# Counting the SBUF port that VectorE and GpSimd share in a kernel's own scheduler

## The chip, the cores and the metric

The kernel runs on one core of a Trainium2 chip. The metric is the device time of one execution in microseconds. A core has TensorE (matrix products), VectorE, ScalarE and GpSimd (elementwise work) and SyncE, which here issues the DMAs. GpSimd reads and writes SBUF only; the results of matmuls lie in PSUM and are read by VectorE and ScalarE.

## The reference

Causal attention with a bias from running sums, then two feed-forward layers, all in 32-bit floats, for 4 sequences of 576 tokens, 8 heads of 64:

```python
scores = (q @ k^T) / sqrt(64)
cum    = cumsum(max(s, 0))
scores = where(causal, -1e9, scores + min(-(cum[:, None] - cum[None, :]), 0))
attn   = exp(scores - rowmax); attn = attn / (rowsum + 1e-9)
x      = attn @ v                              # 2304 tokens x 512
x      = ((x @ w_a) * (x @ w_b)) @ w_out       # 512 -> 1536 -> 512
h      = x @ w_in                              # 512 -> 2048
out    = (max(h, 0) + alpha * min(h, 0)) @ w_out2
```

## The kernel before

**Tiles and stages.** The 2304 tokens are cut into four blocks of 512 and a last one of 256. For each block, `ffn(blk)` (L901) runs both feed-forward layers; between its matmuls the steps of the attention of the next block are interleaved (`attention(blk)`, L738). The attention of the first sequence runs alone at the start (`first_attention`, L693). TensorE's work is in its own order in the program text.

**Exact products.** A 32-bit product is made of three products of split operands (`mm3`, L893): each operand is split into a high part and a low part by `split` (L266): a copy into the type fp32r, mostly on ScalarE (L239), and a subtraction `lo = src - hi` (L252, `sub`). For weights these are the tiles wh and wl, for gated activations gh and gl, for the layer's input xh and xl. wl and gl are computed from SBUF, so VectorE or GpSimd can do them; xl is computed from PSUM, so VectorE does it.

**Weights.** There are 68 weight tiles of 128x512. They arrive as 64-bit floats. While block 0 is computed, `decode` (L802) turns each into 32-bit: one scaling on ScalarE (L810) or GpSimd (L812), then on VectorE one shift (a TENSOR_SCALAR w<-w) and two combines (SCALAR_TENSOR_TENSOR w<-raw,w), all three issued through `dve` (L245). The result sits in one of four w32 buffers until it is split and stored to the DRAM tensor w_d; blocks 1 to 4 read it back from there (raw<-w_d). The buffers of wh and wl are six each.

**Softmax.** Per head and row block: VectorE reduces scores out of PSUM (L245, z<-bank), ScalarE takes the exponential (L232), VectorE makes the reciprocal of the sums (sm), and `scale` (L257) multiplies the rows by it, on GpSimd or VectorE. `scale` also multiplies by alpha in the second layer (m). GpSimd masks the diagonal (L490). In later blocks VectorE or ScalarE adds the bias (L480, L484).

**The order of the work.** Everything that is not TensorE's is a chain of steps (Python generators). A step yields a dictionary of engines with a planned duration in ns, and the class `Order` simulates them while the program is being built: `_first` (L121) takes the step that can start earliest, ties going to the earlier due time, and `_run` (L136) emits it on an engine. So the scheduler fixes each engine's instruction order and, where a dictionary names two engines, which of them gets the instruction. The first engine of a dictionary is kept unless another one would end the step sooner by more than `late`: 1000 ns (LATE), 1300 ns in block 0 (LATE_0). Each engine is a resource of its own: `free[e]` is when it is next free. On the chip the engines run these orders and wait for each other by semaphores.

Of the kernel before, what the change touches and what calls it, by code (L numbers as in the profile page):

```python
# [13 lines left out]
ALU = mybir.AluOpType  # L14
# [10 lines left out]
SIGN = -(1 << 31)  # L25
# [47 lines left out]
        self.free, self.waiting = n, []  # L73


class Order:


# [42 lines left out]
    def _first(self):  # L121

        best = None
        for link in self.open:
            due, n, c, (engines, _) = link
            end, late = None, 0.0
            for e, t in engines.items():
                at = max(c.time, self.free.get(e, 0.0)) + t
                if end is None or at + late < end:
                    end, eng, start = at, e, at - t  # L130
                late = self.late
            if best is None or (start, due, n) < best[:3]:
                best = start, due, n, link, eng, end
        return best

    def _run(self, first):  # L136
        _, _, _, link, eng, end = first
        self.open.remove(link)
        c, (_, wait) = link[2:]
        self.free[eng] = end  # L140
        c.time = end + wait
        self._next(c, eng)

# [29 lines left out]
def attention_two_moe_kernel(  # L173
# [10 lines left out]
    nc = tc.nc  # L184
# [7 lines left out]
    WN = 512  # L192
# [25 lines left out]
            engines={ENGINES.PE, ENGINES.Activation, ENGINES.DVE, ENGINES.Pool, ENGINES.SP}  # L218
# [6 lines left out]
    SEEN = 100  # L225

    def size(ap):
        return prod(ap.shape[1:])

    def act(o, i, func=AF.Copy, **k):  # L230
        yield {"act": 90 + 0.833 * size(o) + 93 * len(set(k) - {"scale"})}, SEEN
        nc.scalar.activation(o, i, func, **k)  # L232

    def copy(o, i, rate):

        n = size(o)
        eng = yield {"act": 90 + 0.833 * n, "dve": 70 + rate * n}, SEEN
        if eng == "act":
            nc.scalar.activation(o, i, AF.Copy)  # L239
        else:  # L240
            nc.vector.tensor_copy(o, i)

    def dve(n, rate, f, *args, **k):
        yield {"dve": 70 + rate * n}, SEEN
        f(*args, **k)  # L245

    def sub(o, i0, i1, sbuf=True):
        n = size(o)
        engines = {"pool": 115 + 2.17 * n} if sbuf else {}
        engines["dve"] = 70 + 1.04 * n  # L250
        eng = yield engines, SEEN
        (nc.vector if eng == "dve" else nc.gpsimd).tensor_tensor(o, i0, i1, op=ALU.subtract)  # L252

    def scale(o, i, s0, s1):
        n = size(o)
        eng = yield {"pool": 115 + 1.09 * n, "dve": 70 + 0.52 * n}, SEEN
        (nc.vector if eng == "dve" else nc.gpsimd).tensor_scalar(  # L257
            o, i, s0, s1, op0=ALU.mult, op1=ALU.mult
        )

# [186 lines left out]
    def z_space(r, b, h):  # L447

        if b == 0 and r < 4 and h // 2 % 3 == 2:
            return {0: (gp, "gh", 3), 2: (gp, "gl", 3), 3: (ft, "t", 4)}[r] + (of_early[r],)  # L450
        return work, f"z{r}", 1 if r == 4 else 4, of_z[r]

    def biases(b, h, rs):

        r = rs[-1]
        got = []
        first = b < SUMS_PE and r < 4
        cb, ready = (None, None) if first else cb_t[b, h, r // 4]  # L460
        col = b * H // 2 + h if r == 4 else b * H + h
        pool, tag, bufs, slots = z_space(rs[0], b, h)

        def chain():
            if not first:
                yield ready
            yield slots
            z = pool.tile([P, sum(min(S, P * (i + 1)) for i in rs)], F32, name="z", tag=tag,
                          bufs=bufs)
            got.append(z)  # L470
            c = 0
            if first:
                return
            for i in rs:
                n = min(S, P * (i + 1))
                o, q = z[:, c:c + n], cumq[:, i, col:col + 1]
                both = {"act": 180 + 0.833 * n, "dve": 70 + 0.52 * n}
                eng = yield dict(sorted(both.items(), reverse=not scarce)), SEEN
                if eng == "dve":
                    nc.vector.tensor_scalar(  # L480
                        o, cb[0][:, 0:n], q, 0.0, op0=ALU.add, op1=ALU.min
                    )
                else:
                    nc.scalar.activation(o, cb[0][:, 0:n], AF.Identity, bias=q)  # L484
                c += n
            if r >= 3:
                run.give(of_c1 if r == 4 else of_c0, run.t)

            def keep(d, pattern):
                nc.gpsimd.affine_select(  # L490
                    d, d, pattern=pattern, base=0, channel_multiplier=1, compare_op=ALU.is_ge,
                    fill=MASKED,
                )

            if r == 4:
                for j in range(2):
                    yield {"pool": 120 + 1.09 * QB}, SEEN
                    keep(z[j * QB:(j + 1) * QB, QA:S], [[-1, QB]])
            else:
                k = len(rs)  # L500
                yield {"pool": 120 + 1.09 * P * k}, SEEN
                d = z.rearrange("p (c n) -> p c n", n=P)
                keep(d[:, 0:3:2, :] if k == 2 else d[:, r:r + 1, :], [[0, k], [-1, P]])

        z_t[b, h, rs[0]] = got, run.spawn(chain(), slack=SL_BIAS)

    def both(b, hp, rs):
# [3 lines left out]
    def soften(b, h, rs, srcs, *banks_read):  # L511

        got, masked = z_t[b, h, rs[0]]
        run.need(masked)
        z = got[0]
        k = len(rs)
        mn = small.tile([P, 2], F32, name="mn", tag="mn")
        sm = small.tile([P, 2], F32, name="sm", tag="sm")
        parts = []
        c = 0  # L520
        for i in rs:
            n = min(S, P * (i + 1))
            parts.append(z[:, c:c + n])
            c += n

        def rest():
            for i, p in enumerate(parts):
                yield from act(
                    p, p, AF.Exp, bias=mn[:, i:i + 1], scale=-1.0, accum_out=sm[:, i:i + 1]
                )  # L530
            for i in range(k):
                yield from dve(
                    1, 1, nc.vector.tensor_scalar, sm[:, i:i + 1], sm[:, i:i + 1], 1e-9, None,
                    op0=ALU.add,
                )
            yield from dve(1, 1, nc.vector.reciprocal, sm[:, 0:k], sm[:, 0:k])
            for i, p in enumerate(parts):
                yield from scale(p, p, sm[:, i:i + 1], 1.0)

        def first():  # L540
            c = 0
            for i, src in enumerate(srcs):
                n = src.shape[-1]
                p = z[:, c:c + n]
                yield from dve(
                    n, 1.04, nc.vector.tensor_tensor_reduce, p, src,
                    mask[:, QA - n:] if b < SUMS_PE and rs[0] < 4 else p, -0.125, BIG, ALU.add,
                    ALU.min, mn[:, i:i + 1],
                )
                c += n  # L550
            if len(parts) < len(srcs):
                yield from dve(
                    1, 1, nc.vector.tensor_tensor, mn[:, 0:1], mn[:, 0:1], mn[:, 1:2],
                    op=ALU.min,
                )
            z_t[b, h, rs[0]] = z, run.spawn(rest(), run.t)

        got = run.spawn(first())
        z_t[b, h, rs[0]] = z, got
        for i in banks_read:  # L560
            reader[i] = got
# [240 lines left out]
    def decode(r, w):  # L802

        r2 = r.rearrange("p (n t) -> p n t", t=2)
        low, high = r2[:, :, 0], r2[:, :, 1]
        wf = f32(w)
        ts, stt = nc.vector.tensor_scalar, nc.vector.scalar_tensor_tensor
        eng = yield {"act": 517, "pool": 590}, SEEN
        if eng == "act":
            nc.scalar.activation(wf, high.bitcast(F32), AF.Copy, scale=REBIAS)  # L810
        else:
            nc.gpsimd.tensor_scalar(  # L812
                wf, high.bitcast(F32), REBIAS, 1.0, op0=ALU.mult, op1=ALU.mult
            )
        yield from dve(WN, 0.52, ts, w, w, 3, None, op0=ALU.logical_shift_left)
        yield from dve(WN, 1.04, stt, w, high, SIGN, w, op0=ALU.bitwise_and, op1=ALU.bitwise_or)
        yield from dve(
            WN, 1.04, stt, w, low, 29, w, op0=ALU.logical_shift_right, op1=ALU.bitwise_or
        )

    def load_pair(i):
# [199 lines left out]
    for blk in range(NB):  # L1021
# [8 lines left out]
        if 1 <= blk < NB - 1:  # L1030
            n = max(0, blk * S + QA - blocks[blk + 1][0])
# [4 lines left out]
        for i, _ in enumerate(ffn(blk)):  # L1036
            want = min(len(steps), (i + 1) * len(steps) * FASTER / total)
            while done < want:
                f, args = steps[done]
# [64 lines left out]
```

## Time and profile before

| | |
|---|---|
| time, median of 3 runs | 1090.11 us (1083.55 to 1091.57) |
| the profiled execution: its time / its span | 1084.09 / 1082.3 us |
| TensorE busy | 1040.2 us, 96% of the span |
| VectorE busy | 564.4 us, 52% |
| ScalarE busy | 568.0 us, 52% |
| GpSimd busy | 661.2 us, 61% |
| subtractions (L252) on GpSimd: wl from w / wl from raw / gl | 56 / 215 / 90 |

The span runs from the first to the last instruction. PE is TensorE, DVE VectorE, ACT ScalarE, POOL GpSimd, SP SyncE, L252 a line of the program. An instruction's busy time runs from its start to its end, and time in which it is held up after its start counts as busy. Busy spans of neighbours on one engine can overlap a little, since the end of one and the start of the next do.

### The profile page before, as it was taken

Reading aid. Unit: us, or ns where it says so; the run is one execution under the profiler, and the core shown is the slowest. Engines: PE = TensorE matmul, PEld = TensorE weight load, DVE = VectorE, ACT = ScalarE, POOL = GpSimd, SP = SyncE. Lnnn points to the kernel's source line nnn. Section 1 sums busy time; section 2 is a strip of 40 time slices with the busy share of each in tenths; the row PEclk is TensorE's granted clock in tenths of the full one; section 3 lists DMA queues with packets and bytes.
Section 4 is the critical chain, followed back from the end, with each engine's and each line's share of the span. In section 5 each row is a group of like instructions: output and inputs, shape, how many; then the busy total and the mean of one; then the engine's idle time right before and its main releaser. Section 6 shows DMA issues by size and latency. Waiting matters only on the chain.

```text
span 1082.3 us, 15995 instructions
## 1 busy us (share of the span) xinstructions
PE 1040.2 (96%) x5413; PEld 817.5 (76%) x5413; DVE 564.4 (52%) x1233; ACT 568.0 (52%) x1187; POOL 661.2 (61%) x664
## 2 busy tenths in 40 slices
PE   6889899888999999999999999999999999999998
PEld 5467677666777777777777777777788888889987
DVE  6989889889835333543445343543222233433443
ACT  6755555655555545554455445455443444446564
POOL 3666536566767545666566655655544456667997
PEclk9989999989999999999999999999999999999999
DMA  7675856745667243435256343423163243216551
GB/s 221 203 238 180 279 210 220 259 167 200 220 187 224 82 136 103 134 105 161 59 147 181 74 145 96 137 81 111 49 202 126 88 129 98 79 58 234 182 169 40
DMA packets 87394, 162.68 MB, mean 150 GB/s; under 512 B 7120, under 2 KB 24528, under 8 KB 87312
## 3 DMA queue, kind: packets, MB, share of 16 engines
q1 hardware_dynamic: 87312, 161.66, 47.0%
q8 instruction: 42, 0.69, 0.3%
q14 instruction: 40, 0.33, 0.1%
HBM read 139.02 MB, written 22.62 MB: 149 GB/s over the span
## 4 chain that ended last, share of the span: by engine, by line
PE 74%; DVE 11%; issue 6%; POOL 5%; ACT 2%; DMA 1%; SPq 0%; POOLq 0%; DVEq 0%; ACTq 0%
PE bank L894 17%; PE bank L895 16%; PE bank L896 16%; DVE w L245 7%; PE bank L1003 5%; PE bank L1005 5%; PE bank L1004 5%; PE bank L439 3%; PE bank L633 3%; POOL wl L252 3%; PE bank L613 2%; DVE z L245 1%; PE bank L586 1%; PE bank L682 1%; POOL m L257 1%
## 5 line engine op out<-in xcount | busy, mean ns | idle before, releaser
L252 POOL TENSOR_TENSOR wl<-raw,wh 128x512 fp32r<-128x512 f32 x215 | 280.2, 1309 | 164.8 <-ACT wh L239 144.5
L894 PE MATMUL bank<-xh,wh 128*128 128x512 f32 (+1 forms) x800 | 306.8, 384 | 0.4 <-DVE g L245 0.4
L896 PE MATMUL bank<-xh,wl 128*128 128x512 f32 (+1 forms) x800 | 296.3, 370 | 0.0
L895 PE MATMUL bank<-xl,wh 128*128 128x512 f32 (+1 forms) x800 | 295.8, 370 | 0.0
L239 ACT ACTIVATE wh<-raw 128x512 fp32r<-128x512 f32 x266 | 166.8, 627 | 107.9 <-PE bank L895 50.7
L894 PEld LDWEIGHTS bank<-xh,wh 128*128 128x128 f32 x800 | 151.3, 189 | 40.3 <-issue 13.9
L896 PEld LDWEIGHTS bank<-xh,wl 128*128 128x128 f32 x800 | 151.3, 189 | 26.6
L895 PEld LDWEIGHTS bank<-xl,wh 128*128 128x128 f32 x800 | 151.5, 189 | 23.1
L252 POOL TENSOR_TENSOR gl<-g,gh 128x512 fp32r<-128x512 f32 (+1 forms) x90 | 118.3, 1314 | 46.4 <-ACT gh L239 46.3
L257 POOL TENSOR_SCALAR z<-z,sm 128x128 f32<-128x128 f32 (+4 forms) x133 | 90.4, 689 | 85.8 <-DVE sm L245 58.4
L239 ACT ACTIVATE gh<-g 128x512 fp32r<-128x512 f32 (+1 forms) x140 | 82.2, 587 | 91.4 <-DVE g L245 90.8
L245 DVE SCALAR_TENSOR_TENSOR w<-raw,w 128x512 int32<-128x512 int32 x136 | 128.4, 951 | 2.6
L245 DVE SCALAR_TENSOR_TENSOR g<-bank,m 128x512 f32<-128x512 f32 (+1 forms) x80 | 50.9, 636 | 131.9 <-POOL m L257 131.8
L1003 PE MATMUL bank<-wh,gh 128*128 128x512 f32 x288 | 117.6, 408 | 0.2 <-ACT gh L239 0.2
L1005 PE MATMUL bank<-wh,gl 128*128 128x512 f32 x288 | 113.7, 395 | 0.4 <-POOL gl L252 0.2
L1004 PE MATMUL bank<-wl,gh 128*128 128x512 f32 x288 | 113.3, 393 | 0.0
L252 POOL TENSOR_TENSOR wl<-w,wh 128x512 fp32r<-128x512 f32 x56 | 84.5, 1511 | 44.3 <-ACT wh L239 38.8
L245 DVE TENSOR_TENSOR g<-bank,a_sb 128x512 f32<-128x512 f32 (+1 forms) x60 | 38.1, 635 | 140.7 <-PE bank L896 131.3
L232 ACT ACTIVATE z<-z,mn 128x128 f32<-128x128 f32 (+4 forms) x144 | 82.9, 578 | 52.6 <-DVE mn L245 52.5
L257 POOL TENSOR_SCALAR m<-m,alpha_sb 128x512 f32<-128x512 f32 (+1 forms) x78 | 59.9, 768 | 60.9 <-ACT m L232 60.3
L894 PE MATMUL bank<-gh,wh 128*128 128x512 f32 (+1 forms) x240 | 93.5, 390 | 2.9 <-ACT gh L239 2.9
L895 PE MATMUL bank<-gl,wh 128*128 128x512 f32 (+1 forms) x240 | 89.3, 372 | 2.5 <-POOL gl L252 1.5
(77 smaller groups left out, 1469.3 us busy)
## 6 DMA issues: line engine op xcount, KB each, us to landing
raw<-w_d SPq DMA_DIRECT2D x136, 512.0 KB, 3.9
raw<-in_w_dram SPq DMA_DIRECT2D x68, 512.0 KB, 4.4
w_d<-w SPq DMA_DIRECT2D x68, 256.0 KB, 2.3
kq<-in_kq_a_dram SPq DMA_DIRECT2D x32, 256.0 KB, 5.3
vb<-in_v_dram SPq DMA_DIRECT2D x32, 256.0 KB, 5.2
kq<-in_kq_b_dram SPq DMA_DIRECT2D x16, 352.0 KB, 4.3
cb<-cum_d SPq DMA_DIRECT2D x32, 144.0 KB, 5.8
out_dram<-o SPq DMA_DIRECT2D x18, 256.0 KB, 2.6
```

The costliest lines, as they stand in the source:

```text
L232: nc.scalar.activation(o, i, func, **k)
L239: nc.scalar.activation(o, i, AF.Copy)
L245: f(*args, **k)
L252: (nc.vector if eng == "dve" else nc.gpsimd).tensor_tensor(o, i0, i1, op=ALU.subtract)
L257: (nc.vector if eng == "dve" else nc.gpsimd).tensor_scalar(o, i, s0, s1, op0=ALU.mult, op1=ALU.mult)
L439: nc.tensor.matmul(dst[j], got[0][o, QA + r * P:QA + n], got[0][o, 0:n], start=b >= SUMS_PE, stop=True)
L894: nc.tensor.matmul(o, wh, ih, start=first, stop=False)
L895: nc.tensor.matmul(o, wh, il, start=False, stop=False)
L896: nc.tensor.matmul(o, wl, ih, start=False, stop=last)
L1003: nc.tensor.matmul(acc[t], gh[:, c], wh, start=first, stop=False)
L1004: nc.tensor.matmul(acc[t], gh[:, c], wl, start=False, stop=False)
L1005: nc.tensor.matmul(acc[t], gl[:, c], wh, start=False, stop=last)
```

## The change

A second resource, "port", is held in the plan together with the engine: every GpSimd step holds ("pool", "port"), and a new name for VectorE, "dve2", holds ("dve", "port"). Steps of VectorE that read SBUF on both sides, or copy or scale within SBUF, are now called "dve2": the decode's shift and combines, subtractions and scalings from SBUF, the bias of L480, the copy within SBUF and the minimum of two columns. Those that read PSUM stay "dve". For subtractions and scalings the fixed `late` is replaced by 0.95 of the difference between the two planned durations.

```diff
+HOLDS = {"pool": ("pool", "port"), "dve2": ("dve", "port")}
+class Either(dict):
+    @property
+    def late(self):
+        return 0.95 * (self["pool"] - self["dve2"])
+def holds(e):
+    return HOLDS.get(e, (e,))
@@ Order._first
             for e, t in engines.items():
-                at = max(c.time, self.free.get(e, 0.0)) + t
+                at = max(c.time, *(self.free.get(x, 0.0) for x in holds(e))) + t
                 if end is None or at + late < end:
                     end, eng, start = at, e, at - t
-                late = self.late
+                late = getattr(engines, "late", self.late)
@@ Order._run
-        self.free[eng] = end
+        for x in holds(eng):
+            self.free[x] = end
@@ helpers
     def copy(o, i, rate):
...
-        eng = yield {"act": 90 + 0.833 * n, "dve": 70 + rate * n}, SEEN
+        vector = "dve" if rate > 1 else "dve2"
+        eng = yield {"act": 90 + 0.833 * n, vector: 70 + rate * n}, SEEN
...
-    def dve(n, rate, f, *args, **k):
-        yield {"dve": 70 + rate * n}, SEEN
+    def dve(n, rate, f, *args, port=False, **k):
+        yield {"dve2" if port else "dve": 70 + rate * n}, SEEN
...
     def sub(o, i0, i1, sbuf=True):
         n = size(o)
-        engines = {"pool": 115 + 2.17 * n} if sbuf else {}
-        engines["dve"] = 70 + 1.04 * n
-        eng = yield engines, SEEN
-        (nc.vector if eng == "dve" else nc.gpsimd).tensor_tensor(o, i0, i1, op=ALU.subtract)
+        t = 70 + 1.04 * n
+        eng = yield Either(pool=115 + 2.17 * n, dve2=t) if sbuf else {"dve": t}, SEEN
+        (nc.gpsimd if eng == "pool" else nc.vector).tensor_tensor(o, i0, i1, op=ALU.subtract)
     def scale(o, i, s0, s1):
...
-        eng = yield {"pool": 115 + 1.09 * n, "dve": 70 + 0.52 * n}, SEEN
+        eng = yield Either(pool=115 + 1.09 * n, dve2=70 + 0.52 * n), SEEN
@@ biases (L477)
-                both = {"act": 180 + 0.833 * n, "dve": 70 + 0.52 * n}
+                both = {"act": 180 + 0.833 * n, "dve2": 70 + 0.52 * n}
@@ soften: minimum of two columns
-                    op=ALU.min,
+                    op=ALU.min, port=True,
@@ decode: the shift and both combines
-        yield from dve(WN, 0.52, ts, w, w, 3, None, op0=ALU.logical_shift_left)
+        yield from dve(WN, 0.52, ts, w, w, 3, None, op0=ALU.logical_shift_left,
+                       port=True)
...
```

## Rows read from the trace of the kernel before

**Rows 1.** Windows: stretch, its length; each engine's busy us (instructions); clock; DMA.
```profile
core 0: us, PE busy (x) PEld busy (x) DVE busy (x) ACT busy (x) POOL busy (x), PEclk, DMA share, GB/s
60.00:320.50 260.50, 238.68 (x1167) 182.17 (x1167) 222.79 (x382) 147.79 (x302) 160.38 (x135) 0.97 0.64 216
30.00:307.00 277.00, 250.50 (x1267) 186.09 (x1267) 244.12 (x455) 163.53 (x349) 170.91 (x149) 0.96 0.66 221
320.50:976.60 656.10, 655.62 (x3214) 511.93 (x3213) 251.02 (x611) 317.02 (x643) 380.29 (x402) 1.00 0.39 117
976.60:1082.30 105.70, 99.96 (x727) 93.40 (x725) 43.93 (x58) 61.94 (x129) 91.39 (x82) 0.99 0.47 160
```

**Rows 2.** First feed-forward matmul (L895); output stores of blocks 0 and 1 (start, us).
```profile
L895 PE MATMUL bank<-xl,wh x800: 280/389/628, 60.1 to 1072.8; 128*128 128x512 f32 x128, 128*128 128x256 f32 x32
...
320.54 1.75 SPq L263 DMA_DIRECT2D out_dram<-o  x3
...
550.23 1.99 SPq L263 DMA_DIRECT2D out_dram<-o  x3
```

**Rows 3.** Groups by shape, VectorE, 30 to 307 us: count | busy us, mean ns | idle before.
```profile
L245 DVE SCALAR_TENSOR_TENSOR w<-raw,w 128x512 int32<-128x512 int32 x136 | 128.4, 951 | 2.6
L245 DVE TENSOR_SCALAR w<-w 128x512 int32<-128x512 int32 x68 | 44.4, 655 | 12.3 <-ACT w L810 12.0 <-POOL w L812 0.4
L252 DVE TENSOR_TENSOR wl<-w,wh 128x512 fp32r<-128x512 f32 x12 | 17.8, 1498 | 5.2 <-ACT wh L239 5.1
...
L252 DVE TENSOR_TENSOR gl<-g,gh 128x512 fp32r<-128x512 f32 x4 | 4.6, 1148 | 0.4 <-ACT gh L239 0.4
```

**Rows 4.** Instructions of tiles w and g, whole span: ns min/median/max, first and last start.
```profile
L245 DVE SCALAR_TENSOR_TENSOR w<-raw,w x136: 666/693/1783, 34.4 to 306.6; 128x512 int32<-128x512 int32 x136
L245 DVE TENSOR_SCALAR w<-w x68: 402/421/1520, 34.0 to 305.4; 128x512 int32<-128x512 int32 x68
...
L252 DVE TENSOR_TENSOR wl<-w,wh x12: 716/1366/3110, 47.9 to 300.7; 128x512 fp32r<-128x512 f32 x12
...
L245 DVE SCALAR_TENSOR_TENSOR g<-bank,m x80: 423/691/695, 209.6 to 1075.6; 128x512 f32<-128x512 f32 x64, 128x256 f32<-128x256 f32 x16
```

**Rows 5.** Timeline: start us, us, engine, line, operation (VectorE, then GpSimd).
```profile
182.84 3.11 DVE L252 TENSOR_TENSOR wl<-w,wh 128x512 fp32r<-128x512 f32 x1 [0.54 <-ACT wh L239]
...
182.85 1.29 POOL L252 TENSOR_TENSOR wl<-w,wh 128x512 fp32r<-128x512 f32 x1
184.10 1.29 POOL L252 TENSOR_TENSOR gl<-g,gh 128x512 fp32r<-128x512 f32 x1
```

**Rows 6.** Windows of L252 on GpSimd alone: stretch, length, busy us (instructions).
```profile
30.00:307.00 277.00, 115.69 (x77) 0.96 0.66 221
...
307.00:976.60 669.60, 282.32 (x219) 1.00 0.38 117
```

**Rows 7.** Windows of L257 on GpSimd alone.
```profile
30.00:307.00 277.00, 48.07 (x58) 0.96 0.66 221
```

**Rows 8.** Timeline of VectorE: a combine and the instruction behind it.
```profile
146.06 0.69 DVE L245 SCALAR_TENSOR_TENSOR w<-raw,w 128x512 int32<-128x512 int32 x1
146.67 0.15 DVE L245 TENSOR_SCALAR sm<-sm 128x1 f32<-128x1 f32 x1
```

**Rows 9.** Waits (60 to 320.5 us; last row VectorE's, 30 to 307): us, times, longest.
```profile
ACT w L810 <- POOL wl L252: 43.9, 33, 2.6
...
DVE w L245 <- ACT w L810: 12.0, 11, 2.3
...
DVE wl L252 <- ACT wh L239: 5.1, 6, 1.2
```

**Rows 10.** Waits of TensorE and its weight loads for GpSimd, 0 to 60 us.
```profile
PEld bank L613 <- POOL z L257: 7.2, 6, 2.8
...
PE bank L613 <- POOL z L257: 4.2, 2, 2.6
```

**Rows 11.** Timeline of TensorE: the last matmul.
```profile
1078.11 0.39 PE L1005 MATMUL bank<-wh,gl 128*128 128x512 f32 x1
```

More of the change, by code (lines that the diff above doesn't have):

```diff
@@ L248, in sub @@
         n = size(o)
-        engines = {"pool": 115 + 2.17 * n} if sbuf else {}
-        engines["dve"] = 70 + 1.04 * n
-        eng = yield engines, SEEN
-        (nc.vector if eng == "dve" else nc.gpsimd).tensor_tensor(o, i0, i1, op=ALU.subtract)
+        t = 70 + 1.04 * n
+        eng = yield Either(pool=115 + 2.17 * n, dve2=t) if sbuf else {"dve": t}, SEEN
+        (nc.gpsimd if eng == "pool" else nc.vector).tensor_tensor(o, i0, i1, op=ALU.subtract)
     def scale(o, i, s0, s1):
         n = size(o)
-        eng = yield {"pool": 115 + 1.09 * n, "dve": 70 + 0.52 * n}, SEEN
-        (nc.vector if eng == "dve" else nc.gpsimd).tensor_scalar(
+        eng = yield Either(pool=115 + 1.09 * n, dve2=70 + 0.52 * n), SEEN
+        (nc.gpsimd if eng == "pool" else nc.vector).tensor_scalar(
             o, i, s0, s1, op0=ALU.mult, op1=ALU.mult
@@ L476, in chain @@
                 o, q = z[:, c:c + n], cumq[:, i, col:col + 1]
-                both = {"act": 180 + 0.833 * n, "dve": 70 + 0.52 * n}
+                both = {"act": 180 + 0.833 * n, "dve2": 70 + 0.52 * n}
                 eng = yield dict(sorted(both.items(), reverse=not scarce)), SEEN
-                if eng == "dve":
+                if eng == "dve2":
                     nc.vector.tensor_scalar(
@@ L814, in decode @@
             )
-        yield from dve(WN, 0.52, ts, w, w, 3, None, op0=ALU.logical_shift_left)
-        yield from dve(WN, 1.04, stt, w, high, SIGN, w, op0=ALU.bitwise_and, op1=ALU.bitwise_or)
+        yield from dve(WN, 0.52, ts, w, w, 3, None, op0=ALU.logical_shift_left,
+                       port=True)
+        yield from dve(WN, 1.04, stt, w, high, SIGN, w, op0=ALU.bitwise_and, op1=ALU.bitwise_or,
+                       port=True)
         yield from dve(
-            WN, 1.04, stt, w, low, 29, w, op0=ALU.logical_shift_right, op1=ALU.bitwise_or
+            WN, 1.04, stt, w, low, 29, w, op0=ALU.logical_shift_right, op1=ALU.bitwise_or,
+            port=True
         )
```

## The prediction

> **What bounds the kernel now.** I read the views in this order: busy time by stretch, the groups of instructions by shape, the spread of single instructions, the waits, and last the end of the chain. By stretch [rows 1], TensorE is busy 655.62 of the 656.10 us between 320.5 and 976.6, and 99.96 of the 105.70 us after that. So only the first 320 us have room. Token block 0 runs from 60.1 to 320.5, which is 260.4 us; block 1 takes 229.7 us [rows 2] for the same matrix work without the short matmuls of L429 and L433, for which I allow some 4 us by estimate. About 26 us is therefore all that block 0 can give. TensorE is idle 260.50 - 238.68 = 21.8 us of it, and its granted clock is 0.97 there and 1.00 later. In block 0 each of the 68 weight tiles is also decoded on VectorE: one shift and two combines. From 30 to 307 us VectorE is busy 244.12 of 277 us, and GpSimd 170.91.
>
> VectorE's busy time there is not all work. A combine (SCALAR_TENSOR_TENSOR w<-raw,w) lasts 951 ns in the mean [rows 3], but half of all 136 last 693 ns or less, and the longest 1783 [rows 4]. The gate's product, of the same 128x512 size with one operand in PSUM, never passes 695 ns [rows 4]. So what stretches is the instruction with its operands in SBUF. [rows 5] show one case: a subtraction on VectorE begins at 182.84, two GpSimd subtractions run from 182.85 to 185.39, and VectorE's ends at 185.95, after 3.11 us instead of 0.72.
>
> **The change, part by part.** It adds no instruction and drops none; it reorders them and moves subtractions (L252) and scalings (L257) from GpSimd to VectorE. Before, GpSimd kept one unless VectorE would end it 1000 ns sooner (1300 in block 0). Now VectorE takes it if it ends sooner by more than 0.95 of the planned difference: 592 ns for 128x512, where the difference is 623. Both wait for the same port in the plan, so VectorE takes all that become ready unless it is itself in an instruction that needs no port (reductions from PSUM, gates, small columns). Of VectorE's 244.12 us in the stretch the groups of [rows 3], which use the port, are 195; the other 49 are under a fifth of 277. So I let GpSimd keep a fifth. The other marks (decode, the minimum of two columns, the bias of L480) tell the plan of the port and move nothing by themselves. SyncE issues the same transfers; a subtraction that ends sooner frees its raw or w32 buffer sooner, and the DMA engines, at 0.64 of their time in block 0 [rows 1], have room for a load that starts earlier.
>
> *Block 0, stall that goes.* Against the uncontended durations: combines 136 x (951 - 693) = 35.1 us; shifts 68 x (655 - 421) = 15.9; weight subtractions 12 x (1498 - 716) = 9.4; gl 4 x (1148 - 716) = 1.7 [rows 3, 4]. Together 62 us of VectorE time.
>
> *Block 0, work that comes.* GpSimd has 77 subtractions and 58 scalings there, 115.69 and 48.07 us [rows 6, 7]. Four fifths are 62 and 46. A full-size two-operand instruction on VectorE steps by 146.67 - 146.06 = 0.61 us when it meets nobody [rows 8]; the busy 0.69 overlaps the next. 62 x 0.61 = 38 us. A full-size scaling is like the shift, 0.42 us; the softmax ones are a quarter to four quarters of that width, so 0.35 in the mean by estimate, 46 x 0.35 = 16. Together 54 us.
>
> *Block 0, stall that stays.* Lower bound 0: the chip keeps to the planned order. Upper bound: the two engines meet by chance as now. GpSimd's time falls to a fifth, and VectorE's instructions on the port rise from 220 to 328, so 62 x 0.2 x 1.49 = 18 us. I take 6, nearer to 0: the plan's prices (602 and 1226 ns) are close to the steps measured (0.61 us here, 184.10 - 182.85 = 1.25 on GpSimd [rows 5, 8]), so the planned order should mostly hold. VectorE's sum is -62 + 54 + 6 = -2 us, between -8 and +10.
>
> Here a rule can be weighed. The row shows that VectorE's subtraction lost 3.11 - 0.72 = 2.39 us behind two GpSimd instructions in a row [rows 5]. The Trainium skill (SBUF — State Buffer, Who interferes with whom) calls the shared pair an exclusive lock: the one that starts first has it for its whole instruction and the other blocks, so a wait would end with the instruction in its way. By the rule this wait would have been at most 1.25 us, half of it; the stall that stays would halve with it, to 3 us, and the whole sum would be 1069 in place of 1072 us. The row decides.
>
> *Block 0, waits.* ScalarE's first decode step waits 43.9 us for GpSimd's weight subtraction, which frees one of four w32 buffers, and VectorE's shift waits 12.0 us for that step [rows 9]. The subtraction shrinks from 1.5 to about 0.7 us, and the 12.0 us come as 11 waits of 1.1 us: I take 9 of the 12 off (bounds 0 and 12). Against it, a subtraction on VectorE waits there for ScalarE's wh, with reductions, gates and decodes queued behind it, and TensorE's PSUM banks behind those. The 12 now on VectorE waited 5.1 us, 0.43 each [rows 9]. For 50 more weight subtractions that is 21 us at most, and 0 where VectorE is late anyway. VectorE is busy 88% of the stretch, so I take 3. Block 0 comes to -2 - 9 + 3 = -8 us.
>
> *First attention (0 to 60).* TensorE's transposes and their loads wait 7.2 + 4.2 = 11.4 us for scalings on GpSimd [rows 10]. On VectorE one takes about half as long, but from 30 us on it also decodes there. I take -3 (bounds -6 and 0).
>
> *Blocks 1 to 3: nothing.* 0.8 of 219 subtractions [rows 6] at 0.61 us put 107 us more on VectorE, which is then busy some 360 of 656 us. TensorE covers it; without that cover each wait at the head of VectorE's queue would cost its 0.43 us.
>
> *Last block.* It has half as many tokens per weight, and GpSimd is busy 91.39 of 105.70 us [rows 1] beside a nearly full TensorE. The last matmul ends at 1078.5 of 1082.3 [rows 11], and that tail of 3.8 us stays. Of the 5.74 us idle, about 2 are left: I take -1 (0 to -2).
>
> **Sum.** -8 - 3 + 0 - 1 = -12 us on the profiled execution's own 1084.09 us: 1072 us. That execution is 6 us below the median of the three runs (1090.11), so a median may stand a few us above the sum.
>
> **Rivals.** *The order holds fully.* No stall stays, waits in front of VectorE vanish, and block 0 comes down to TensorE's own pace: -26 - 3 - 1 = -30, 1054 us. For it: the port's load in the plan falls by more than half of GpSimd's 164 us. Against: VectorE still has 244 - 62 + 54 = 236 us of work in 277.
>
> *VectorE is as full as before: no change.* Stall is only exchanged for work (-62 + 54 + 8), the shorter decode loop is eaten by the waits for ScalarE: 1084 us, with 1080 to 1090 around it. For it: the first three terms nearly cancel. Against: the buffer waits of [rows 9] and the first attention. The Trainium skill speaks for this one (Perfetto Trace Analysis, Optimizing Scalar/DVE Operations): the two engines share a port, so "offloading operations between those two might not help". The trace agrees that they block each other; it does not show yet what moving work the other way gives.
>
> *Slower: VectorE queues behind ScalarE.* If each moved weight subtraction holds VectorE for its full 0.43 us (+21) and the stall stays at the chance level (+18 in place of 6), block 0 comes to -62 + 54 + 18 - 9 + 21 = +22 us, less 4 elsewhere: 1102 us. It decides from the point where those waits pass 11 us with the rest of my sum. For it: VectorE is the fuller of the two engines and now gets more. Against: planned times agree with measured ones, and a late VectorE does not wait.
>
> **How the numbers follow.** Forecast 0.46, order holds fully 0.16, no change 0.22, slower 0.16. About 1% (11 us) is what a measurement of this kernel can tell from no change. My forecast lies just past that line; two thirds of its chance is beyond it (0.31) and a third within (0.15). Faster by over 1%: 0.31 + 0.16 = 0.47. Slower by over 1%: 0.15. Within: 0.38. The forecast's own range, by its bounds, is 1060 to 1080. The range for 8 in 10 reaches to the full-order case, 1054, and into the slower one, to 1094.
>
> **What would show it.** In the new profile: combines at 0.69 to 0.75 us in the mean rather than 0.95; GpSimd under 250 us busy in all, VectorE near 700; 50 or more weight subtractions on VectorE before 307 us; block 0's first output before 312 us; blocks 1 to 3 unchanged at 656 us within 2. I would be wrong if combines stayed above 0.85 us (order not kept), if VectorE's waits for ScalarE's wh passed 11 us in block 0, or if TensorE lost its full load after 320 us.

## The result, and the profile after

The changed kernel takes 1053.76 us (median of four runs, 1050.13 to 1055.80) beside 1089.57 for the kernel before. The ratio is 0.9677, with a 95% interval from 0.9627 to 0.9726: 35 us faster. The forecast was 12 us, 1072; the time lies a quarter of a microsecond below 1054, the lower end of the range for 8 in 10. The profiled execution has a span of 1048.4 us.

The same windows as in [rows 1], cut at the new block ends (stretch, length; busy us and count of each engine; clock; DMA):

```profile
core 0: us, PE busy (x) PEld busy (x) DVE busy (x) ACT busy (x) POOL busy (x), PEclk, DMA share, GB/s
0.00:60.00 60.00, 49.22 (x326) 34.29 (x327) 48.88 (x210) 45.25 (x125) 13.28 (x30) 0.97 0.74 210
30.00:280.00 250.00, 245.50 (x1302) 185.10 (x1299) 226.40 (x557) 167.38 (x356) 44.16 (x47) 1.00 0.76 242
56.50:290.30 233.80, 230.64 (x1167) 177.57 (x1167) 210.53 (x479) 149.68 (x304) 43.02 (x46) 1.00 0.76 245
...
290.00:943.00 653.00, 653.00 (x3203) 510.02 (x3202) 362.11 (x866) 317.80 (x643) 110.42 (x146) 1.00 0.39 118
943.00:1048.40 105.40, 101.38 (x738) 95.97 (x737) 67.24 (x128) 63.44 (x130) 15.65 (x13) 1.00 0.50 160
```

The first feed-forward matmul (an answer by tile: ns min/median/max, first and last start in us), then SyncE's timeline with the first stores of blocks 0, 1 and 3, against [rows 2]:

```profile
L916 PE MATMUL bank<-xl,wh x800: 278/389/398, 56.5 to 1040.0; 128*128 128x512 f32 x128, 128*128 128x256 f32 x32
```

```profile
290.32 1.93 SPq L281 DMA_DIRECT2D out_dram<-o  x3
...
520.01 2.62 SPq L281 DMA_DIRECT2D out_dram<-o  x3
...
945.70 1.69 SPq L281 DMA_DIRECT2D out_dram<-o  x3
```

The reader sees where the time went. The stage ahead of block 0 ends at 56.5 us in place of 60.1 (-3.6). Block 0 takes 290.3 - 56.5 = 233.8 us in place of 260.4 (-26.6). Blocks 1 to 3 take 655.4 us, as before (656.1), with TensorE busy 653.00 of 653.00. From the store of block 3 to the end there are 102.7 us in place of 105.7 (-3.0). In block 0 TensorE is now nearly full and its granted clock is 1.00. Of the 26.6 us, 18.6 are idle time of TensorE that is gone (21.8 us before [rows 1], 3.2 now); the other 8.0 are its own busy time, 238.68 us before and 230.64 now for the same 1167 matmuls, with the granted clock at 0.97 before.

VectorE's groups by shape, 30 to 280 us, against 30 to 307 before ([rows 3]; the window ends one decode short: 67 of 68 shifts, 134 of 136 combines); then GpSimd's:

```profile
L264 DVE SCALAR_TENSOR_TENSOR w<-raw,w 128x512 int32<-128x512 int32 x134 | 91.6, 705 | 0.1
L270 DVE TENSOR_TENSOR wl<-w,wh 128x512 fp32r<-128x512 f32 x43 | 30.4, 716 | 3.5 <-ACT wh L258 3.4
L264 DVE TENSOR_SCALAR w<-w 128x512 int32<-128x512 int32 x67 | 27.5, 420 | 5.9 <-ACT w L828 5.8
L270 DVE TENSOR_TENSOR gl<-g,gh 128x512 fp32r<-128x512 f32 x24 | 18.2, 760 | 1.1 <-ACT gh L258 0.9
...
L270 POOL TENSOR_TENSOR wl<-w,wh 128x512 fp32r<-128x512 f32 x23 | 31.3, 1363 | 164.1 <-ACT wh L258 149.5 <-PE bank L604 10.5 <-DMA w_d<-w 3.9
L270 POOL TENSOR_TENSOR gl<-g,gh 128x512 fp32r<-128x512 f32 x2 | 2.6, 1322 | 5.1 <-ACT gh L258 5.1
```

A combine takes 705 ns (before 951), a shift 420 (655), a weight subtraction on VectorE 716 (1498). GpSimd has 25 of the subtractions left there and is busy 44.16 us; before it was 170.91 in the longer stretch.

### The profile page after: what moved, and what is told of

It is laid out like the page before. It is cut to its first block, busy times and chain, and to the rows that moved or that the text cites. A ratio compares the mean times of both kernels' runs of the same rounds, so it can differ in the third digit from the quotient of the medians.

```text
span 1048.4 us, 15810 instructions
## 1 busy us (share of the span) xinstructions
PE 1030.4 (98%) x5413; PEld 814.8 (78%) x5413; DVE 685.0 (65%) x1664; ACT 572.4 (55%) x1192; POOL 180.1 (17%) x228
## 4 chain that ended last, share of the span: by engine, by line
PE 85%; DVE 8%; DMA 4%; ACT 1%; issue 1%; SPq 0%; POOL 0%; ACTq 0%; DVEq 0%; POOLq 0%
PE bank L915 19%; PE bank L917 18%; PE bank L916 18%; PE bank L1024 6%; PE bank L1026 6%; PE bank L1025 5%; PE bank L457 3%; DVE w L264 3%; PE bank L631 3%; DMA w_d<-w 3%; PE bank L651 2%; PE bank L604 1%; DVE z L264 1%; PE bank L700 1%; DVE wl L270 1%
## 5 line engine op out<-in xcount | busy, mean ns | idle before, releaser
L270 DVE TENSOR_TENSOR wl<-raw,wh 128x512 fp32r<-128x512 f32 x209 | 145.0, 695 | 153.6 <-ACT wh L258 150.3
L270 POOL TENSOR_TENSOR wl<-raw,wh 128x512 fp32r<-128x512 f32 x63 | 82.0, 1302 | 333.4 <-ACT wh L258 317.2
L270 DVE TENSOR_TENSOR gl<-g,gh 128x512 fp32r<-128x512 f32 (+1 forms) x132 | 91.5, 693 | 44.6 <-ACT gh L258 41.9
L258 ACT ACTIVATE gh<-g 128x512 fp32r<-128x512 f32 (+1 forms) x140 | 82.2, 587 | 64.2 <-DVE g L264 60.1
L264 DVE SCALAR_TENSOR_TENSOR w<-raw,w 128x512 int32<-128x512 int32 x136 | 93.3, 708 | 0.1
L917 PE MATMUL bank<-gh,wl 128*128 128x512 f32 (+1 forms) x240 | 88.9, 370 | 0.0
L275 DVE TENSOR_SCALAR m<-m,alpha_sb 128x512 f32<-128x512 f32 (+1 forms) x75 | 35.1, 467 | 66.6 <-ACT m L250 65.7
L250 ACT ACTIVATE m<-bank 128x512 f32<-128x512 f32 (+1 forms) x80 | 44.2, 552 | 57.8 <-PE bank L917 57.4
L258 ACT ACTIVATE pt<-bank 128x384 f32<-128x384 f32 (+1 forms) x96 | 48.9, 524 | 42.2 <-PE bank L631 41.4
```

The source lines that it names most:

```text
L270: (nc.gpsimd if eng == "pool" else nc.vector).tensor_tensor(o, i0, i1, op=ALU.subtract)
L275: (nc.gpsimd if eng == "pool" else nc.vector).tensor_scalar(o, i, s0, s1, op0=ALU.mult, op1=ALU.mult)
L917: nc.tensor.matmul(o, wl, ih, start=False, stop=last)
```

## The experiments

Two theories. *Order*: the plan knows of the port, so it puts instructions that use it at times when the other engine does not. *Assignment*: GpSimd simply does less on the port, whatever the order. The rivals of the prediction stand beside them: VectorE as the limit, and waits for ScalarE. Times are medians, ratios are to the kernel before on the same chip.

**The port without the new rule.**

```diff
-        eng = yield Either(pool=115 + 2.17 * n, dve2=t) if sbuf else {"dve": t}, SEEN
+        eng = yield {"pool": 115 + 2.17 * n, "dve2": t} if sbuf else {"dve": t}, SEEN
-        eng = yield Either(pool=115 + 1.09 * n, dve2=70 + 0.52 * n), SEEN
+        eng = yield {"pool": 115 + 1.09 * n, "dve2": 70 + 0.52 * n}, SEEN
```

> The plan counts the port, but subtractions and scalings keep the old rule (GpSimd unless VectorE ends 1000 or 1300 ns sooner). Order theory (the gain is that planned order keeps the two engines apart): combines near 0.71 us in the mean as in the changed kernel (before: 0.95), and a good part of the gain, 1060 to 1072 us. Assignment theory (the gain is GpSimd's shorter time on the port): no gain, 1080 to 1095 us, since GpSimd still holds the port for some 160 us of block 0.

1119.88 us, ratio 1.0287 (1.0268 to 1.0305): 31 us slower, beyond what either theory expected. GpSimd's group and VectorE's, by shape, over the whole run:

```profile
L270 POOL TENSOR_TENSOR wl<-w,wh 128x512 fp32r<-128x512 f32 x68 | 93.3, 1378 | 61.6 <-ACT wh L258 49.0 <-issue 11.4 <-POOL z L275 1.0
...
L264 DVE TENSOR_SCALAR w<-w 128x512 int32<-128x512 int32 x68 | 43.6, 645 | 32.0 <-ACT w L828 31.1 <-POOL w L830 0.8
```

All 68 weight subtractions went to GpSimd, 56 did before. That follows from the code: once both engines wait for one port in the plan, VectorE can end a full-size subtraction at most 623 ns sooner, which is never 1000. So the port needs the new rule. The shift then waits 31.1 us for ScalarE (12.0 before [rows 9]).

**The new rule without the port.**

```diff
-HOLDS = {"pool": ("pool", "port"), "dve2": ("dve", "port")}
+HOLDS = {"dve2": ("dve",)}
```

> The new rule for subtractions and scalings, but the plan knows no port. Order theory: the engines meet by chance, combines at 0.80 us or more in the mean, 1066 to 1080 us. Assignment theory: GpSimd's time on the port is down to about a quarter whatever the plan knows, so 1050 to 1058 us and combines at 0.75 us or less.

1073.37 us, ratio 0.9856 (0.9832 to 0.9879): less than half the gain. Its groups:

```profile
L264 DVE SCALAR_TENSOR_TENSOR w<-raw,w 128x512 int32<-128x512 int32 x136 | 120.0, 892 | 1.8
...
L270 POOL TENSOR_TENSOR wl<-w,wh 128x512 fp32r<-128x512 f32 x39 | 58.5, 1500 | 64.0 <-ACT wh L258 58.4 <-DVE m L275 2.8 <-DVE mn L264 1.4
```

This looks like the order theory, but order is not all that differs. Without the port the plan finds GpSimd free while VectorE decodes and gives it 39 of the 68 weight subtractions; the changed kernel gives it 24. So order and engines had to be parted.

**The engines fixed, the port taken away or added.** In two kernels each subtraction and scaling is put by a list on the engine that it has in another kernel, and only the plan's knowledge of the port differs (here the engines of the changed kernel, without the port):

```diff
-HOLDS = {"pool": ("pool", "port"), "dve2": ("dve", "port")}
+HOLDS = {"dve2": ("dve",)}
+ON_GPSIMD = {
...
-        eng = yield Either(pool=115 + 2.17 * n, dve2=t) if sbuf else {"dve": t}, SEEN
+        fixed = {"pool": 115 + 2.17 * n} if key in ON_GPSIMD else {"dve2": t}
+        eng = yield fixed if sbuf else {"dve": t}, SEEN
...
```

> Each subtraction and scaling stays on the engine it has in the changed kernel (566 on VectorE, 138 on GpSimd), but the plan that orders them knows no port. Order theory: 1062 to 1072 us, near the rule alone (1073), with combines over 0.75 us in the mean. Assignment theory: 1050 to 1057 us, as the changed kernel.

1057.11 us, ratio 0.9717 (0.9690 to 0.9744), combines 752 ns: the time is on the edge of what the assignment theory expected, the combines are on the edge of what the order theory did. The two were timed again beside each other:

> The changed kernel itself, beside the next run on one chip. Both theories: ratio 0.965 to 0.973 to the kernel before.

> The changed kernel's engines, ordered by a plan without the port, once more. If order has a share of its own: 3 to 9 us over the changed kernel on the same chip (block 0 was 8 us longer in the profile, the medians 3 apart). If it has none: within 2 us.

The changed kernel 1051.29 us (1049.84 to 1053.75), ratio 0.9666 (0.9642 to 0.9689); its engines without the port 1059.19 us (1055.07 to 1060.43), ratio 0.9729 (0.9705 to 0.9754). The runs do not overlap. Of 35.6 us on this chip, 27.7 come with the engines alone and 7.9 with the order. The earlier medians, not taken beside each other, put the order's share at 3.4 (1057.11 and 1053.76). VectorE's groups of the second, over the whole run, and then its window:

```profile
L289 DVE SCALAR_TENSOR_TENSOR w<-raw,w 128x512 int32<-128x512 int32 x136 | 99.2, 743 | 0.8
...
L296 DVE TENSOR_TENSOR wl<-w,wh 128x512 fp32r<-128x512 f32 x44 | 34.6, 787 | 1.2 <-ACT wh L283 1.2
...
L289 DVE TENSOR_SCALAR w<-w 128x512 int32<-128x512 int32 x68 | 29.6, 439 | 7.6 <-ACT w L855 4.8 <-DMA cb<-cum_d 2.7
```

```profile
30.00:280.00 250.00, 239.06 (x1237) 180.22 (x1234) 235.38 (x554) 162.15 (x346) 59.48 (x53) 0.98 0.72 235
```

Without the order the combine is 743 ns, 35 over the 708 of the changed kernel over its whole run, and VectorE is busy 235.38 us from 30 to 280 in place of 226.40.

The other corner: the engines of the kernel before, with the port.

> Each subtraction and scaling stays on the engine it has in the kernel before (132 on VectorE, 572 on GpSimd), and the plan counts the port. If the port alone was slow at 1120 us because its rule sent all 68 of block 0's weight subtractions to GpSimd: 1085 to 1100 us here. If it is slow because a port that is full in the plan makes VectorE's other work wait in line: 1105 to 1125 us. A pure order theory wants under 1075 us.

1093.95 us, ratio 1.0058 (1.0037 to 1.0079): no gain, a slight loss. This is what the first of the two explanations expected: most of the 31 us that the port alone cost came with the engines that the old rule chose.

Its window, the combines over the whole run, and VectorE's longest wait from 30 to 307 us, here and in the kernel before:

```profile
30.00:307.00 277.00, 247.61 (x1234) 181.10 (x1232) 208.45 (x445) 164.09 (x343) 157.04 (x146) 0.96 0.68 215
```

```profile
L362 DVE SCALAR_TENSOR_TENSOR w<-raw,w 128x512 int32<-128x512 int32 x136 | 115.6, 880 | 0.0
```

```profile
DVE g L362 <- POOL m L375: 16.1, 11, 3.7
...
DVE g L245 <- POOL m L257: 2.9, 5, 1.0
```

To 307 us VectorE is busy 208.45 us in place of 244.12, but the combine is still 880 ns and block 0 takes 270.8 us in place of 260.4. While GpSimd is busy for 157 of 277 us, order alone keeps the engines apart only in part. VectorE now waits instead: its gates wait 16.1 us for GpSimd's scalings, before 2.9.

**All on VectorE.**

```diff
-        eng = yield Either(pool=115 + 2.17 * n, dve2=t) if sbuf else {"dve": t}, SEEN
+        eng = yield {"dve2": t} if sbuf else {"dve": t}, SEEN
...
```

> All subtractions and scalings from SBUF on VectorE; GpSimd keeps the masks and a few decodes. No collisions are left either way. If VectorE paces block 0, GpSimd's last 25 subtractions and 10 scalings there cost it about 19 us: 1062 to 1073 us. If TensorE paces block 0 of the changed kernel: within 1% of it, 1050 to 1060 us. If any use of GpSimd beside VectorE is a loss: below 1048 us.

1057.92 us, ratio 0.9717 (0.9696 to 0.9739). Neither a combine nor a weight subtraction is longer than 694 ns (tile w, min/median/max), and block 0 takes 238.5 us against 233.8:

```profile
L264 DVE SCALAR_TENSOR_TENSOR w<-raw,w x136: 670/684/693, 37.9 to 289.6; 128x512 int32<-128x512 int32 x136
...
L270 DVE TENSOR_TENSOR wl<-w,wh x68: 665/684/694, 43.7 to 291.3; 128x512 fp32r<-128x512 f32 x68
```

So GpSimd's share beside VectorE is worth a few microseconds, not more.

**More VectorE work.** One shift by 0 is added to each decode, in the kernel before and in the changed one (there with `port=True`):

```diff
+        yield from dve(WN, 0.52, ts, w, w, 0, None, op0=ALU.logical_shift_left)
```

> The kernel before with one more shift (by 0) in each of the 68 decodes: 0.42 us each if it meets nobody, 28 us of VectorE in block 0, known to the plan. If VectorE's time paces block 0 of the kernel before: 1112 us or more against 1084 (each shift also collides). If a wait for another engine paces it: under 1098 us.

> The changed kernel with one more shift (by 0) in each decode, 28 us of VectorE in block 0, known to the plan. If TensorE paces block 0 there and VectorE, busy 226 of 250 us, has room: at most 10 us over the changed kernel (under 1064). If VectorE still paces it: 20 us or more (over 1074). The same padding cost the kernel before 18 us by the medians.

1107.42 us in the kernel before, 18.5 over it, between the two expectations. In the changed kernel 1074.25 us, 20.5 over it, just past the bound for "VectorE still paces it": its block 0, though TensorE is nearly full, has little slack on VectorE. In both, two thirds or more of the added 28 us show in the end.

**GpSimd's extra work: reading or writing.** Behind each decode GpSimd does useless work that nobody waits for and that the plan does not know of:

```diff
+        nc.gpsimd.tensor_tensor(spare, mask, mask, op=ALU.subtract)
```

> The changed kernel, and behind each decode GpSimd subtracts one constant 128x512 tile from itself into a spare tile that nobody reads: 68 x 1.25 = 85 us more of GpSimd in block 0, of which the plan knows nothing. Port theory (time of GpSimd on the port is what costs): about half of what GpSimd held before comes back, 25 to 38 us: 1077 to 1092 us, combines over 0.80 us. Chain theory (the gain is a shorter way from decode to split, buffers free sooner): within 6 us of the changed kernel.

```diff
+        for _ in range(2):
+            nc.gpsimd.memset(spare, 0.0)
```

> As the run with GpSimd's extra reads, but the extra work is 136 memsets of the spare tile, some 0.53 us each, 72 us in all: GpSimd writes SBUF and reads nothing. If only GpSimd's reads meet VectorE: within 6 us of the changed kernel, combines at 0.72 us. If any use of SBUF by GpSimd does: 20 us or more. If what costs is the delay of GpSimd's own queue: as much as with the reads.

Reading: 1087.24 us, ratio 1.0008 (0.9985 to 1.0032); the whole gain is gone. Writing: 1058.64 us, ratio 0.9745 (0.9698 to 0.9792). GpSimd is as busy in both from 30 to 280 us. The window and the groups with the reads:

```profile
30.00:280.00 250.00, 227.68 (x1154) 168.35 (x1151) 241.27 (x513) 149.91 (x319) 115.03 (x103) 0.96 0.64 208
```

```profile
L264 DVE SCALAR_TENSOR_TENSOR w<-raw,w 128x512 int32<-128x512 int32 x136 | 109.5, 826 | 0.1
L264 DVE TENSOR_SCALAR w<-w 128x512 int32<-128x512 int32 x68 | 36.2, 544 | 1.8 <-ACT w L829 1.8
...
L842 POOL TENSOR_TENSOR spare<-mask 128x512 f32<-128x512 f32 x68 | 85.4, 1255 | 3.6
```

And with the writes:

```profile
30.00:280.00 250.00, 238.88 (x1249) 179.14 (x1248) 228.93 (x535) 160.62 (x342) 114.45 (x171) 0.99 0.73 236
```

```profile
L264 DVE SCALAR_TENSOR_TENSOR w<-raw,w 128x512 int32<-128x512 int32 x136 | 92.4, 700 | 0.1
L264 DVE TENSOR_SCALAR w<-w 128x512 int32<-128x512 int32 x68 | 36.1, 541 | 4.3 <-ACT w L829 4.3
...
L843 POOL MEMSET spare<- 128x512 f32 x136 | 77.6, 571 | 6.6
```

So it is not GpSimd's queue, and not a shorter way from decode to split: 85 us of GpSimd instructions that read SBUF, with no consumer, cost as much as the change gains. The chain theory expected under 6 us. The writes cost 5 us by the medians and 7 by the ratios to the kernel before; the shifts alone, 68 x (541 - 420), are 8 us more of VectorE.

**Variants.** Scalings back under the old rule (the second pair of lines of the first diff):

> The changed kernel with scalings (L275) back under the old rule, GpSimd unless VectorE ends 1000 or 1300 ns sooner; subtractions and the port stay. If the subtractions carry the gain (GpSimd's 116 of 164 us in block 0): 1058 to 1066 us. If scalings, which TensorE's transposes wait for, carry it: over 1070 us.

1065.15 us, ratio 0.9793 (0.9748 to 0.9839): with the scalings under the old rule some 21 us of the gain are left (17 to 27 by the interval), so the scalings bring the rest. The factor 0.95 at 0.5, and five w32 buffers in place of four:

```diff
-        return 0.95 * (self["pool"] - self["dve2"])
+        return 0.5 * (self["pool"] - self["dve2"])
```

> The factor 0.95 at 0.5: VectorE takes a subtraction when GpSimd could start it up to 312 ns earlier. Between the changed kernel and all on VectorE: 1050 to 1058 us. If GpSimd's last third of block 0's weight subtractions is still too much: under 1050.

```diff
-    W32, RAW, KQ, VB, CB = 4, 6, 3, 4, 3
+    W32, RAW, KQ, VB, CB = 5, 6, 3, 4, 3
```

> The changed kernel with five w32 buffers for decoded weights in place of four: ScalarE's decode waits 15.5 us in block 0 for the store that frees one. If TensorE paces block 0: the same within 3 us of the changed kernel (1051 to 1057). If the stores hold the decode back: 4 to 8 us less (1046 to 1050).

1057.05 us, ratio 0.9728 (0.9699 to 0.9757), and 1055.92 us, ratio 0.9710 (0.9682 to 0.9739). Neither beats the changed kernel; no version here does.

## Why the prediction was wrong, point by point

**What bounds.** Right. Only the first 320 us had room; block 0 could give about 26 us and gave 26.6, blocks 1 to 3 behind it did not move, and the last one gave 3.0 of the 5.7 us in which TensorE was idle there. The signs named in the prediction came too (combines at 705 ns, GpSimd 180 us busy in all and VectorE 685, block 0's first output at 290.3), but they could not tell a gain of 12 us from one of 35.

**The stall that goes, and that stays.** The mechanism is shown: GpSimd's reads bring it back, GpSimd's writes bring back only the shifts' part. The stall that stays was put at 6 us, and 6 stayed. With 684 ns for a combine and a weight subtraction that meet nobody and 685 for gl (the medians of the run with all on VectorE), it is 134 x (705 - 684) = 2.8, 43 x (716 - 684) = 1.4 and 24 x (760 - 685) = 1.8. The upper bound, 18 us by chance, stands too: with the same engines and no port in the plan it is 136 x (743 - 684) = 8.0 for combines, 68 x (439 - 420) = 1.3 for shifts and 44 x (787 - 684) = 4.5 for weight subtractions, some 14 us without gl.

The rule of the lock was weighed on one row, and that row is an exception. In [rows 4] no combine lost more than 1783 - 693 = 1.09 us and no shift more than 1520 - 421 = 1.10, less than the 1.25 us of one GpSimd subtraction. In the trace before, no other VectorE subtraction from w or g lost more than 1.1 us; the 2.39 us of [rows 5] stand alone. So nearly every wait was already short enough for one GpSimd instruction, and the rule gave no ground to halve the stall. Why that one wait took two is not shown.

**The work that comes.** Put at 54 us for 62 subtractions and 46 scalings. In the windows shown 51 and 49 came (43 - 12 and 24 - 4; 53 - 4). Of all 155 such instructions in the stretch GpSimd kept 35 (25 and 10), near the fifth; the prediction had taken the fifth of GpSimd's own 135 alone.

**The failed step: VectorE's sum, and in it the size of the stall that goes.** I made the sum -2 us, between -8 and +10. In the windows shown VectorE's busy time went from 244.12 to 226.40, -18 us, though the second window ends one decode short. Over the same work, from the first shift to the end of the last combine, it went from 241.7 us (of 273.4) to 225.6 (of 248.7): -16, beyond my own bounds.

The two traces give each term over that work in one measure: what an instruction adds on VectorE behind the end of the one before it.

- The work that comes is right: 31 weight subtractions, 21 gl and 46 scalings more add 53.7 us, for a forecast of 54.
- The stall that goes is not. Net of the 6 that stays I had -62 + 6 = -56 us; it is -72. The 136 combines went from 124.9 to 85.4 us, the 68 shifts from 40.2 to 23.5. The 16 subtractions that VectorE had before lost 11.4.
- 4 of the 72 come from instructions that I had left out of the sum: four minima of two columns (684 ns each before, 290 now) and four scalings on VectorE (1.04 us each before).
- All other instructions add 1.7 us, and -72 + 54 + 2 = -16.

So the term that was too small is the 62. Beside the 4 us left out, the main reason is that I mixed two measures: I charged the moved work by its step (0.61 us, not the 0.69 it lasts) and credited the stall by durations, 951 - 693. But an instruction that is held up overlaps its neighbour less. Before, a combine began on average 33 ns ahead of the end of the instruction in front of it; now it is 79. For combines and shifts together that is 7 us, which no duration shows. The last 4 or so are the part of the 6 us of stall that fell on moved instructions, where it is in the 53.7, and the median of 693 that I subtracted, which was itself a little stretched (683 now).

**The waits.** Put at -6 us (-9 + 3). VectorE's idle time in the windows fell from 277 - 244.12 = 32.9 to 250 - 226.40 = 23.6 us, -9.3 (-8.5 from the first shift to the last combine). The shift's wait for ScalarE went from 12.0 to 5.8, not to 3; in its place ScalarE's decode waits 15.5 us for the store that frees a w32 buffer (56.5 to 290.3 us), and a fifth buffer brought nothing:

```profile
ACT w L828 <- DMA w_d<-w: 15.5, 11, 4.5
```

The feared waits of VectorE for wh fell to 3.4 us although 43 subtractions stand there in place of 12. Busy and idle time together make up the shorter window whatever paces it; that VectorE's time still counts there is shown by the added shifts, 20.5 us of 28. TensorE's idle time and clock are in no term of the sum.

**First attention and last block.** -3.6 for a forecast of -3, and -3.0 for -1. What made up these two was not tested.

**The rivals.** "The order holds fully" named the time, 1054, and block 0's end at TensorE's pace; that is in part luck. Some 6 us of stall stayed, and the order has under a quarter of the gain, since the engines alone bring 27.7 of 35.6 us. "No change", where the Trainium skill's sentence stood (Perfetto Trace Analysis, Optimizing Scalar/DVE Operations: offloading between the two engines might not help), fell: here it matters which way work moves, because the same 128x512 subtraction steps by 1.25 us on GpSimd [rows 5] and by 0.65 on VectorE in the changed kernel. "Slower" fell with the 3.4 us that VectorE waits for wh (its point of 11 us was for block 0 alone; with the rest of the sum it is 11 + 4 = 15). The port without the new rule is slower, but through GpSimd. I gave the time that came a chance of 0.16, because I read the sum of VectorE's time and waits as the whole answer and let terms of 60 us cancel to 2.

## What to carry to other kernels

When two engines share something, count what each instruction takes of it, not which engine is less busy: the same subtraction took about twice as long on the engine that looked free. If a scheduler learns of a shared resource, look in the same step at the thresholds that choose between engines: here the old one could no longer be passed. And where large terms cancel in a sum, take each from the same measure (steps, or busy time of the whole engine) and keep the range as wide as their errors.

## What the runs showed of the hardware

GpSimd's writes alone (136 memsets) left VectorE's combine, with two operands in SBUF, at 700 ns, but stretched its shift, with one, from 420 to 541 ns; GpSimd's extra subtractions, which read and write, stretched both, to 826 and 544. The Trainium skill (SBUF — State Buffer, Who interferes with whom) says that a VectorE instruction with two SBUF inputs contends with a GpSimd instruction that reads SBUF and not with one that only writes it; for one in a 2-port mode it says that it contends with GpSimd, without that condition. The rows agree, if the shift is in such a mode, which no run shows directly: it takes 0.42 us where the combine of the same size takes 0.69.
